# Key-value sums on column strips, spread on row strips, and rows transposed 32 at a time on four row strips of TensorE

## The chip, the cores and the metric

The kernel runs on one core of a Trainium2 chip. The core has TensorE for matmuls (PE in the profile, its weight loads PEld), VectorE (DVE), ScalarE (ACT), GpSimd (POOL) and SyncE (SP), which here only starts transfers. Matmuls read SBUF and write PSUM, which has eight banks of 128 partitions by 512 float32. The metric is the device time of one execution, in microseconds; lower is better.

## The reference

The kernel computes two identical layers on x of 2048 rows by 512 (bfloat16): attention with a softmax feature map, without a matrix of rows by rows, then a gated feed-forward part.

```
def A(x, wqkv, w_phi, wo):                 # 32 heads of 16
    q, k, v = split(x @ wqkv)
    pq, pk = q @ w_phi, k @ w_phi          # head by head
    phi_q = concat(softmax(pq), softmax(-pq))
    phi_k = concat(softmax(pk), softmax(-pk))
    kv, z = sum_s phi_k * v, sum_s phi_k
    num = phi_q @ kv
    den = phi_q @ z + 1e-6
    return (num / den) @ wo
def B(x, W_gate, W_up, W_down):            # 512 -> 1376 -> 512
    return (relu(x @ W_gate) * (x @ W_up)) @ W_down
for layer in range(2):
    x = x + A(layernorm(x))
    x = x + B(layernorm(x))
```

## The kernel before

The rows stay in SBUF (`x_sb`) as 16 tiles of 128 rows, worked in four blocks (`st`) of four tiles. Python code lists all operations with what they read and write and an assumed cost. `Program.schedule` then replays them greedily, choosing the order on each engine and a PSUM bank for each `bank(...)`, and `plan` sets the semaphore waits. The order is thus a result of the assumed costs, `occ` and `lat` in nanoseconds; it is fixed in the program, and each engine runs its list in order.

The steps, by function:

- `layernorm(st)` takes statistics on DVE (L435, L436), scales the rows to `ytile` (on DVE at L452; with `early` on ACT at L449) and turns every tile with four 128x128 transposes (helper `tr`, L327) into one bank, which is copied to `yT` in one go: on ACT at L463, with `early` on DVE at L460. There are 15 calls that work on four tiles at once (`step` 4) and one, the very first, that works tile by tile.
- `keys(st)` multiplies each transposed tile by the key and the value weights (`mm`, L323), takes both exponentials on ACT (L487), their sums by head on DVE (L489, L491), and on POOL (L498) makes `vhat`, the values times the reciprocal sums with one column more per head for z, so 17 columns a head. The key-value sums come next: for each of eight groups `g` (sign by quarter of the features) a 128x128 slice of `expk` is multiplied by the 136 columns of `vhat` of its eight heads, over the four tiles: 32 matmuls of 136 columns into three banks. Only the products of a head with itself are wanted, so most of each 128x136 block is not used. Three DVE operations add the banks to `kvsum` (L511, L514).
- `sums()` runs once a layer: it masks `kvsum` into `ZDw` (the weights of the denominators, L523) and `kvbd` (L529), eight DVE operations each.
- `queries(st)` makes `expq` (L539). `attend(st)` computes denominators with 32 matmuls of 16 columns (`ZDw`, `expq`), then the factors `atok`, transposed to `aT`, which must be spread from one row per head to the head's 16 rows. For block 0 this is done on TensorE, with eight matmuls by the constant `EC`; half of the results are multiplied into `expq` on DVE straight from PSUM (L586), the other half by way of a copy on ACT (L590, L591). For the other blocks it is a round trip through DRAM: one write to `scratch` (L575) and eight reads into `abT` (L577) on SP's queue. The numerators are 32 matmuls on 32x32 tiles of the array (L600), copied to `oT`, multiplied by `wo_sb` and added to `x_sb`.
- `glu(st)` is the feed-forward part: matmuls by `Wg`, `Wu` and `Wd`, relu on ACT (L639), product on DVE (L641), residual on DVE (L624).

The first layer's keys of all four blocks come first. Then, per layer, `glu` of one block runs between `out_of_a` of the next one and, in the first layer, `into_a` of the same block for the second layer.

Of the kernel before, what the change touches and what calls it, by code (L numbers as in the profile page):

```python
# [246 lines left out]
def build_kernel(nc, A_x, A_wqkv, A_w_phi, A_wo, W_gate, W_up, W_down, out):  # L247
# [8 lines left out]
    with ExitStack() as ctx:  # L256
# [4 lines left out]
        def sb(name, shape, dt=BF16):  # L261
            return E(nc.sbuf_tensor(name, [P] + list(shape), dt))

        NWARM = 8
        NY, NYT, NE, NV, NG, NH = 4, 6, 5, 4, 3, 18
# [17 lines left out]
        kvsum = sb("kvsum", [8, 136], FP32)  # L283
        kvbd = sb("kvbd", [2, NC, 128])
# [16 lines left out]
        EC = sb("EC", [8, 128])  # L301
        ident = sb("ident", [128])
        mask8a = sb("mask8a", [8])
        mask8 = sb("mask8", [8])
        abT = sb("abT", [8, 512])
        scratch = [nc.dram_tensor(f"spread{i}", (64, 512), BF16, kind="Internal").ap() for i in range(2)]
# [72 lines left out]
        for i in range(NWARM):  # L379
# [8 lines left out]
        op("act", lambda e: e.activation(EC[:].rearrange("p g (h j) -> p (g h) j", j=16), ident[:, 0:64].unsqueeze(2).to_broadcast([P, 64, 16]), ACT.Copy),  # L388
           reads=[R("ident"), R("tables")], writes=[R("EC")], occ=1000, name="EC")

        op("dve", lambda e: e.tensor_tensor(BD.rearrange("p c (h f) -> p c h f", f=16),
# [34 lines left out]
        VIA = lambda c, sg: sg == 1  # L426

        def layernorm(st, step=4, early=False):

            b = cnt["yT"] % NYT  # L430
            cnt["yT"] += 1
            for t0 in range(4 * st, 4 * st + 4, step):
# [9 lines left out]
                if early:  # L442
                    op("dve", (lambda t0: lambda e: e.scalar_tensor_tensor(nmr[:, t0:t0 + step, :], mv[:, t0:t0 + step, 0:1], -1.0, rstd[:, t0:t0 + step, :], ALU.mult, ALU.mult))(t0),
                       reads=Rmv + Ry, writes=[R("nmr", t) for t in ts], occ=75, lat=165, name="nmr")
                for t in ts:
                    yb = cnt["y"] % NY
                    cnt["y"] += 1
# [3 lines left out]
                    else:  # L451
                        op("dve", (lambda t, yb: lambda e: e.tensor_scalar(ytile[:, yb, :], x_sb[:, t, :], mv[:, t, 0:1], rstd[:, t, :], op0=ALU.subtract, op1=ALU.mult))(t, yb),  # L452
                           reads=[R("x", t), R("mv", t), R("rs", t)], writes=[R("y", yb)], occ=322, lat=405, name=f"apply{t}", port=True)
                    ps = bank(f"ytr{t}")
# [4 lines left out]
                    if early:  # L459
                        op("dve", (lambda ps, dst: lambda e: e.tensor_copy(dst, b16half(ps).rearrange("p (c n) -> p c n", c=NC)))(ps, dst),  # L460
                           reads=[ps], writes=[R("yT", b, tt)], occ=331, lat=415, name=f"ycp{t}")
                    else:
                        op("act", (lambda ps, dst: lambda e: e.activation(dst, b16half(ps).rearrange("p (c n) -> p c n", c=NC), ACT.Copy))(ps, dst),  # L463
                           reads=[ps], writes=[R("yT", b, tt)], occ=480, lat=600, name=f"ycp{t}")
            return b

# [3 lines left out]
        def keys(st, b):  # L470

            tiles = []
            for tt in range(4):
                t = 4 * st + tt
                ry = R("yT", b, tt)
# [6 lines left out]
                for ic in range(NC):  # L482
                    mm(pk, full, yT[:, b, ic, tt * 128:(tt + 1) * 128], Wkp[:, ic, :], ic == 0, ic == NC - 1, [ry, R("W", "k", ic)], 512, f"k{t}")
                for ic in range(NC):
                    mm(pv, full, yT[:, b, ic, tt * 128:(tt + 1) * 128], wv[:, ic, :], ic == 0, ic == NC - 1, [ry, R("wv")], 512, f"v{t}")
# [15 lines left out]
            for g0, g1 in ((0, 3), (3, 6), (6, 8)):  # L501
                ps = bank(f"kv{st}{g0}")
                for g in range(g0, g1):
                    sg, c = g // 4, g % 4
                    for j, i in enumerate(tiles):
                        mm(ps, (lambda o: lambda p: p.f32()[:, o:o + 136])((g - g0) * 136), expk[:, i, sg, c * 128:(c + 1) * 128],
# [239 lines left out]
```

## Time and profile before

| | us |
|---|---|
| runs | 424.61, 426.39, 426.71 (median 426.39) |
| the profiled execution, in all | 424.71 |
| its span, first to last instruction | 423.0 |

| group | count | busy us, mean ns of one |
|---|---|---|
| DVE adds to `kvsum`, 408 columns and 272 columns | 12 and 6 | 6.9, 576 and 2.6, 431 |
| DVE writes of `ZDw` and of `kvbd` | 16 and 16 | 1.6, 163 and 3.4, 291 |
| `yT` copies on ACT and on DVE | 52 and 12 | 27.2, 608 and 4.6, 411 |
| spread matmuls (`aT`, `EC`) | 16 | 4.2, 383 |
| write to `scratch`, 64 KB | 6 | lands in 2.0 (median) |

A group's busy time can hold overlaps: matmuls are pipelined, so the next one starts while the last is still draining, and the distance from start to start is shorter than the mean duration. "32\*32" behind an operation is the part of the array that it uses, rows by columns. The granted clock is TensorE's, with 1.00 as full speed.

### The profile page before, as it was taken

What the parts mean: (1) busy time and instruction counts of PE and PEld (TensorE: products, weight loads), DVE (VectorE), ACT (ScalarE), POOL (GpSimd) and SP (SyncE); (2) the same over time, 40 slices, a digit from 0 to 9 for tenths busy, and PEclk for the clock granted to TensorE, in tenths of its full rate; (3) what the DMA queues carried; (4) which work ended last, traced back from release to release, by engine and by line L of the source; (5) the groups of instructions that cost most, each with busy time, mean ns of one, the idle gap of its engine ahead of it and who ended that gap; (6) DMA issues with size and microseconds to landing.
All of it is one profiled execution on the core that took longest, in us unless ns stands there. A gap on an engine that the chain in (4) does not pass through costs nothing.

```text
span 423.0 us, 6858 instructions
## 1 busy us (share of the span) xinstructions
PE 402.1 (95%) x2684; PEld 205.1 (48%) x2731; DVE 275.3 (65%) x587; ACT 213.6 (50%) x432; POOL 69.3 (16%) x71
## 2 busy tenths in 40 slices
PE   7999999599999999999999999977999999999997
PEld 4555555354444545455455445533444544444443
DVE  4999768968479647767774446876932842664332
ACT  5999897655246522834183169855522430342320
POOL 0258780000007000620052008000000000000000
PEclk9999999989999999999999999969999999999999
DMA  8960000330000000200000000022101001301001
GB/s 265 326 210 2 2 0 7 102 107 0 2 0 2 0 2 10 97 0 2 0 2 0 2 2 2 8 99 70 39 1 50 2 0 50 108 2 37 14 0 50
DMA packets 16800, 17.66 MB, mean 42 GB/s; under 512 B 1568, under 2 KB 15744, under 8 KB 16768
## 3 DMA queue, kind: packets, MB, share of 16 engines
q1 hardware_dynamic: 15552, 16.62, 12.0%
q10 hardware_dynamic: 1216, 0.61, 0.5%
q8 instruction: 21, 0.34, 0.3%
q14 instruction: 11, 0.09, 0.1%
HBM read 14.73 MB, written 2.49 MB: 41 GB/s over the span
## 4 chain that ended last, share of the span: by engine, by line
PE 76%; ACT 15%; DVE 6%; DMA 1%; issue 1%; ACTq 0%; DVEq 0%
PE pb L323 72%; ACT expq L539 4%; ACT expk L487 3%; PE pb L327 3%; ACT ytile L449 2%; ACT vsb L495 2%; DMA hT<-in_A_wqkv_dram 1%; DVE expq L591 1%; ACT yT L463 1%; DVE stats L435 1%; PE pb L600 1%; DVE expq L586 1%; DVE Zk L489 1%; ACT Wqp L420 0%; ACT abT L590 0%
## 5 line engine op out<-in xcount | busy, mean ns | idle before, releaser
L639 ACT ACTIVATE gate_sb<-pb 128x512 bf16<-128x512 f32 (+1 forms) x88 | 52.8, 600 | 130.3 <-PE pb L323 130.2
L498 POOL TENSOR_TENSOR vhat<-vsb,rZk 128x544 bf16<-128x544 bf16 x64 | 68.5, 1105 | 193.5 <-DVE rZk L491 187.1
L641 DVE TENSOR_TENSOR hT<-gate_sb,pb 128x512 bf16<-128x512 bf16 (+1 forms) x88 | 59.6, 683 | 52.6 <-PE pb L323 52.3
L323 PE MATMUL pb<-yT,Wu 128*128 128x512 bf16 (+1 forms) x345 | 91.1, 379 | 0.2
L323 PE MATMUL pb<-yT,Wg 128*128 128x512 bf16 (+1 forms) x341 | 90.6, 379 | 0.6
L323 PE MATMUL pb<-Wd,hT 128*128 128x512 bf16 (+3 forms) x355 | 76.8, 372 | 0.4
L624 DVE TENSOR_TENSOR x_sb<-x_sb,pb 128x512 bf16<-128x512 bf16 x55 | 36.4, 685 | 48.6 <-PE pb L323 48.6
L323 PEld LDWEIGHTS pb<-Wd,hT 128*128 128x128 bf16 (+1 forms) x363 | 35.4, 98 | 40.1
L323 PEld LDWEIGHTS pb<-yT,Wu 128*128 128x128 bf16 (+1 forms) x352 | 34.9, 100 | 38.4 <-issue 0.4
L323 PEld LDWEIGHTS pb<-yT,Wg 128*128 128x128 bf16 (+1 forms) x352 | 34.4, 100 | 38.1 <-issue 1.4
L435 DVE BATCH_NORM_STATS2 stats<-x_sb 128x6 f32<-128x512 bf16 x64 | 42.4, 680 | 2.2 <-ACT x_sb L619 1.4
L489 DVE TENSOR_REDUCE Zk<-expk 128x64 f32<-128x1024 bf16 x32 | 38.4, 1204 | 7.7 <-ACT expk L487 7.5
L539 ACT ACTIVATE expq<-pb 128x512 bf16<-128x512 f32 x64 | 35.0, 696 | 12.9 <-PE pb L323 12.9
L487 ACT ACTIVATE expk<-pb 128x512 bf16<-128x512 f32 x64 | 36.3, 639 | 2.3 <-PE pb L323 0.7
L323 PE MATMUL pb<-wo_sb,oT 128*128 128x512 bf16 x121 | 31.9, 399 | 2.2 <-DVE oT L608 1.7
L323 PE MATMUL pb<-wv,yT 128*128 128x512 bf16 x124 | 33.1, 379 | 0.3
L323 PE MATMUL pb<-Wkp,yT 128*128 128x512 bf16 x124 | 32.2, 379 | 0.4 <-DVE yT L460 0.2
L323 PE MATMUL pb<-yT,Wqp 128*128 128x512 bf16 x122 | 30.9, 379 | 0.4 <-ACT Wqp L420 0.2
L463 ACT ACTIVATE yT<-pb 128x512 bf16<-128x512 bf16 x52 | 27.2, 608 | 6.3 <-PE pb L327 6.2
L610 ACT ACTIVATE oT<-pb 128x512 bf16<-128x512 f32 x28 | 15.1, 609 | 24.4 <-PE pb L600 23.6
L591 DVE TENSOR_TENSOR expq<-expq,abT 128x512 bf16<-128x512 bf16 x56 | 21.9, 424 | 8.1 <-DMA abT<-spread 8.1
L323 PE MATMUL pb<-vhat,expk 128*128 128x136 bf16 x256 | 24.4, 223 | 0.2
(68 smaller groups left out, 327.4 us busy)
## 6 DMA issues: line engine op xcount, KB each, us to landing
abT<-spread SPq DMA_DIRECT2D x48, 128.0 KB
out_dram<-x_sb SPq DMA_DIRECT2D x15, 128.0 KB, 1.7
x_sb<-in_A_x_dram SPq DMA_DIRECT2D x3, 512.0 KB, 8.8
Wg<-in_B_W_gate_dram SPq DMA_DIRECT2D x1, 1376.0 KB
Wu<-in_B_W_up_dram SPq DMA_DIRECT2D x1, 1376.0 KB
Wd<-in_B_W_down_dram SPq DMA_DIRECT2D x1, 1280.0 KB
hT<-in_A_wqkv_dram ACTq DMA_DIRECT2D x2, 256.0 KB, 5.8
wv<-in_A_wqkv_dram SPq DMA_DIRECT2D x1, 512.0 KB, 5.8
```

What stands on the lines that cost most here:

```text
L323: op("pe", lambda e: e.matmul(view(ps), lhsT, rhs, start=start, stop=stop), reads=reads, writes=[ps], occ=max(25.0, 0.4167 * n + 2.6), lat ...
L435: op("dve", (lambda t: lambda e: e.bn_stats(stats[:, t, :], x_sb[:, t, :]))(t), reads=[R("x", t)], writes=[R("st", t)], occ=580, lat=680, ...
L463: op("act", (lambda ps, dst: lambda e: e.activation(dst, b16half(ps).rearrange("p (c n) -> p c n", c=NC), ACT.Copy))(ps, dst), reads=[ps], ...
L487: op("act", (lambda i, s, pk: lambda e: e.activation(expk[:, i, s, :], full(pk), ACT.Exp, scale=1.0 - 2.0 * s))(i, s, pk), reads=[pk], wri ...
L489: op("dve", (lambda i, zb: lambda e: e.tensor_reduce(Zk[:, zb, :], expk[:, i, :, :].rearrange("p s (h f) -> p (s h) f", f=16), AX.X, ALU.a ...
L498: op("pool", (lambda i, s, vb, rz: lambda e: e.tensor_tensor(vhat[:, i, s, :, :], vsb[:, vb, :, :], rZk[:, rz, s * 32:(s + 1) * 32].unsque ...
L539: op("act", (lambda c, s, ps: lambda e: e.activation(expq[:, st, c, s, :], full(ps), ACT.Exp, scale=1.0 - 2.0 * s))(c, s, ps), reads=[ps], ...
L591: op("dve", (lambda c, sg, gi: lambda e: e.tensor_tensor(expq[:, st, c, sg, :], expq[:, st, c, sg, :], abT[:, gi, :], ALU.mult))(c, sg, gi ...
L610: op("act", (lambda i, pn: lambda e: e.activation(oT[:, g, i, :], full(pn), ACT.Copy))(i, pn), reads=[pn], writes=[R("oT", g, i)], occ=480 ...
L624: op("dve", lambda e: e.tensor_tensor(x_sb[:, t, :], x_sb[:, t, :], full(ps), ALU.add), reads=[R("x", t), ps], writes=[R("x", t)], occ=597 ...
L639: op("act", (lambda m, gb, pg: lambda e: e.activation(gate_sb[0:m, gb, :], pg.f32()[0:m, :], ACT.Relu))(m, gb, pg), reads=[pg], writes=[R( ...
L641: op("dve", (lambda m, gb, hb, pu: lambda e: e.tensor_tensor(hT[0:m, hb, :], gate_sb[0:m, gb, :], pu.f32()[0:m, :], ALU.mult))(m, gb, hb, pu),
```

## The change

**Key-value sums.** The array is used as four column strips of 32. A strip multiplies the 32 features of two heads by the 34 columns of `vhat` of these two heads, so each 136-column product becomes four of 34 columns, which write 32 partitions each of one bank. All eight groups fit in that bank (272 columns), one operation adds it to `kvsum`. There are 128 matmuls a block, issued as two runs of 64 for two tiles each. `kvsum` shrinks to 8x34 columns and `kvbd` to 32 columns a group.

**Sums.** Three DVE operations in place of sixteen: the epsilon, all of `ZDw`, all of `kvbd`.

**Transposes.** For calls with four tiles, `strips` turns 32 rows of a tile at a time: the four row strips of the array each take their 32 partitions of `ytile` and write to a bank of their own. This makes 64 transposes to 128x32 in one run that starts when all four tiles are scaled, and four copies to `yT`, two on ACT and two on DVE (with `early` four on DVE). A copy holds one strip of all four tiles, so keys of any tile wait for all four. `ytile` has eight buffers in place of four.

**Spread.** `atok` is laid out with 32 columns a quarter, so that `aT` has a quarter's factors on its own 32 partitions. For block 0, the four quarters of one sign are spread at once by four row strips into four banks. The copy by way of ACT is now taken for odd quarters, where it was taken for one sign. The scratch write of the other blocks is all 128 rows of `aT` (128 KB).

```diff
-        NY, NYT, NE, NV, NG, NH = 4, 6, 5, 4, 3, 18
+        NY, NYT, NE, NV, NG, NH = 8, 6, 5, 4, 3, 18
-        kvsum = sb("kvsum", [8, 136], FP32)
-        kvbd = sb("kvbd", [2, NC, 128])
+        kvsum = sb("kvsum", [8, 34], FP32)
+        kvbd = sb("kvbd", [2, NC, 32])
-        EC = sb("EC", [8, 128])
+        EC = sb("EC", [2, 128])
...
-        VIA = lambda c, sg: sg == 1
+        by_tile = set()
+        VIA = lambda c, sg: c % 2 == 1
...
+                    if step == 4:
+                        continue
...
+                if step == 4:
+                    strips(st, b, ybs, early)
             return b
+
+        def strips(st, b, ybs, early):
+            pss = [bank(f"ytr{st}{i}") for i in range(4)]
+            def turn(e):
+                for tt, yb in enumerate(ybs):
+                    for c in range(NC):
+                        for i in range(4):
+                            r = slice(32 * i, 32 * i + 32)
+                            n0 = c * 128 + tt * 32
+                            ins = e.transpose(pss[i].b16()[:, n0:n0 + 32], ytile[r, yb, c * 128:(c + 1) * 128], ident[r, r], tile_position=(32 * i, 0))
+                return ins
+            op("pe", turn, reads=[R("y", yb) for yb in ybs] + [R("ident")], writes=pss, occ=600, lat=800, name=f"ytr{st}")
+            for i in range(4):
...
+                if early or i % 2:
+                    op("dve", (lambda src, dst: lambda e: e.tensor_copy(dst, src()))(src, dst), reads=[pss[i]], writes=[R("yT", b, i), R("ya", b, i)], occ=331, lat=415, name=f"ycp{st}")
+                else:
+                    op("act", (lambda src, dst: lambda e: e.activation(dst, src(), ACT.Copy))(src, dst), reads=[pss[i]], writes=[R("yT", b, i), R("ya", b, i)], occ=480, lat=600, name=f"ycp{st}")
...
-                ry = R("yT", b, tt)
+                ry = [R("yT", b, tt)] + [R("ya", b, i) for i in range(4)] if b in by_tile else R_yT(b)
...
-            for g0, g1 in ((0, 3), (3, 6), (6, 8)):
-                ps = bank(f"kv{st}{g0}")
-                for g in range(g0, g1):
-                    sg, c = g // 4, g % 4
-                    for j, i in enumerate(tiles):
-                        mm(ps, (lambda o: lambda p: p.f32()[:, o:o + 136])((g - g0) * 136), expk[:, i, sg, c * 128:(c + 1) * 128],
-                           vhat[:, i, sg, c * 8:(c + 1) * 8, :], j == 0, j == 3, [R("ek", i, sg), R("vh", i, sg)], 136, f"kv{st}")
...
+            ps = bank(f"kv{st}")
+            def products(js):
+                def fn(e):
+                    for j in js:
+                        for g in range(8):
+                            sg, c = g // 4, g % 4
+                            for i in range(4):
+                                f0 = c * 128 + 32 * i
+                                ins = e.matmul(ps.f32()[32 * i:32 * i + 32, g * 34:g * 34 + 34], expk[:, tiles[j], sg, f0:f0 + 32],
+                                               vhat[:, tiles[j], sg, 8 * c + 2 * i:8 * c + 2 * i + 2, :], start=j == 0 and g == 0, stop=j == 3,
+                                               skip_group_check=True, tile_position=(0, 32 * i))
+                    return ins
+                return fn
+            for js in ((0, 1), (2, 3)):
+                op("pe", products(js), reads=[...],
+                   writes=[ps], occ=500, lat=700, name=f"kv{st}")
...
+            op("dve", lambda e: e.tensor_scalar(kvv[:, 0:4, :, 16], kvv[:, 0:4, :, 16], float(EPS_DEN), None, op0=ALU.add),
+               reads=[R("kvs")], writes=[R("kvs")], occ=70, lat=160, name="eps z")
...
-                dma("sp", lambda e: e.dma_start(scr, aT[0:64, g, :]), reads=[R("aT", g)], writes=[rs], nbytes=65536, name=f"aTo{st}")
+                dma("sp", lambda e: e.dma_start(scr, aT[:, g, :]), reads=[R("aT", g)], writes=[rs], nbytes=131072, name=f"aTo{st}")
...
+        def spread(g, sg):
+            pss = [bank(f"ab0{c}{sg}") for c in range(NC)]
+            def products(e):
+                for c in range(NC):
+                    r = slice(32 * c, 32 * c + 32)
+                    ins = e.matmul(full(pss[c]), EC[r, sg, :], aT[r, g, :], start=True, stop=True, tile_position=(32 * c, 0))
+                return ins
+            op("pe", products, reads=[R("EC"), R("aT", g)], writes=pss, occ=450, lat=650, name="ab0")
+            for c in range(NC):
+                scale_by(0, c, sg, pss[c])
```

## The prediction

> **What bounds the kernel now.** First the page's engine totals and its slices, then busy time by stretch of the span.
>
> ```profile
> span 423.0 us, 6858 instructions
> PE 402.1 (95%) x2684; PEld 205.1 (48%) x2731; DVE 275.3 (65%) x587; ACT 213.6 (50%) x432; POOL 69.3 (16%) x71
> PEclk9999999989999999999999999969999999999999
> ```
>
> ```profile
> 30.00:70.00 40.00, 39.44 (x358) 23.26 (x362) 32.27 (x69) 35.24 (x72) 25.61 (x24) 1.00 0.01 1
> 90.00:270.00 180.00, 178.88 (x1136) 90.88 (x1156) 120.95 (x239) 85.04 (x170) 34.28 (x32) 1.00 0.04 12
> 290.00:420.00 130.00, 128.80 (x693) 61.10 (x704) 64.96 (x126) 40.52 (x76) 0.00 (x0) 1.00 0.10 33
> 70.00:90.00 20.00, 14.77 (x164) 8.07 (x165) 15.79 (x47) 15.38 (x35) 0.00 (x0) 0.91 0.22 72
> 270.00:290.00 20.00, 15.10 (x160) 7.15 (x160) 16.57 (x48) 13.34 (x32) 0.00 (x0) 0.83 0.18 60
> ```
>
> The columns of a stretch are PE, PEld, DVE, ACT, POOL, then granted clock, DMA share and GB/s. In three stretches, 350 of 423 us, TensorE is busy for 99% of the time at full clock, and the starts of its 512-column matmuls lie 0.216 us apart with hardly a gap (four in 0.86 us). There every TensorE nanosecond added or removed moves the end one for one, and what DVE, ACT or POOL gain is worth nothing. Only around 70 to 90 and 270 to 290 us, where a layer's first query block waits for DVE and ACT, does TensorE idle, some 5 us each; before 30 us it idles too. So I count TensorE time, then waits.
>
> The two kinds of work that the change splits are these groups:
>
> ```profile
> L323 PE MATMUL pb<-vhat,expk 128*128 128x136 bf16 x256 | 24.4, 223 | 0.2
> L327 PE MATMUL pb<-ident,ytile 128*128 128x128 bf16 x256 | 22.7, 228 | 1.5 <-DVE ytile L452 1.2 <-DVE kvsum L511 0.2
> L323 PE MATMUL pb<-ZDw,expq 128*128 128x16 bf16 x256 | 9.1, 170 | 3.6 <-ACT expq L539 3.6
> L600 PE MATMUL pb<-expq,kvbd 32*32 32x512 bf16 x256 | 5.6, 409 | 4.2 <-DVE expq L591 4.2
> ```
>
> Their mean durations overlap, so a price is the distance between starts, from the instructions in order of time:
>
> ```profile
> 62.74 0.93 PE L323 MATMUL pb<-vhat,expk 128*128 128x136 bf16 x13
> 63.51 0.38 PE L323 MATMUL pb<-yT,Wqp 128*128 128x512 bf16 x1
> 65.76 2.42 PE L323 MATMUL pb<-ZDw,expq 128*128 128x16 bf16 x90
> ...
> 75.96 0.52 PEld L323 LDWEIGHTS pb<-ZDw,expq 128*128 128x128 bf16 x18 [0.33 <-ACT expq L539]
> 76.50 0.33 PEld L600 LDWEIGHTS pb<-expq,kvbd 32*32 32x32 bf16 x32
> ...
> 121.14 0.19 PEld L600 LDWEIGHTS pb<-expq,kvbd 32*32 32x32 bf16 x32 [0.43 <-issue]
> 121.14 0.65 PE L600 MATMUL pb<-expq,kvbd 32*32 32x512 bf16 x32
> 121.73 0.39 PE L323 MATMUL pb<-yT,Wg 128*128 128x512 bf16 x1
> ...
> 335.14 0.61 PE L327 MATMUL pb<-ident,ytile 128*128 128x128 bf16 x8
> 335.59 0.38 PE L323 MATMUL pb<-yT,Wg 128*128 128x512 bf16 x1
> ```
>
> A key-value product costs (63.51 - 62.74) / 13 = 0.059 us, a transpose (335.59 - 335.14) / 8 = 0.0565, and a 16-column product, the shortest here, (2.42 - 0.17) / 89 = 0.0253.
>
> **Two prices that decide.** (1) The 32 tiled products of L600 are the only tiled ones. The matmul ahead of the run at 121.14 starts at 120.83 and streams until 121.05, so going in costs 0.09 us. Half of its products stream after the other half, the last starts at 121.42 and streams until 121.63, and the next plain matmul starts at 121.73: 0.09 to 0.10 going out. Other runs of L600 in the busy stretches show the same. I take 0.18 us for each change into a tiled form and back. (2) At 121.14, after long matmuls, the 32 weight loads start 3.3 ns apart (0.19 us less one load's 0.09, over 31). At 76.50, after 18 short pairs, the same 32 need 0.33 us: by their single starts the first 28 come 3.3 ns apart and the last four 34 ns apart, with nothing late that they depend on. Around 277.4 us, again after short pairs and with the clock at half, it is 28 quick ones and then 34 ns. I read this as a store of ready instructions, at least 29 pairs of load and matmul deep when full, refilled at one pair in 34 ns whatever the TensorE clock. Against 512-column matmuls the refill is never seen; a long run of short pairs empties the store and then goes at 34 ns. The 90 pairs at 65.76 don't contradict it: 29 + 2.25 / 0.034 = 95.
>
> **The change, part by part.**
>
> Key-value sums: in each of 8 blocks 32 products of 136 columns (32 x 0.059 = 1.89 us) become 128 products of 34 columns, in two runs of 64. By (1) and (2) a run takes 0.18 + (64 - 29) x 0.034 = 1.37 us. 16 x 1.37 - 8 x 1.89 = **+6.8 us**. The trace has no run of 64 tiled pairs, so bounds: from below every pair at the quick 3.3 ns but four tiles at a time sharing the 25.3 ns step, 64 x 0.0063 + 0.18 = 0.58 us a run, -5.8 in all; from above 25.3 ns for every pair, 64 x 0.0253 + 0.18 = 1.80, +13.7. I take 1.37 because the late loads at 76.50 are tiled ones in just this situation.
>
> Transposes: in 15 four-tile calls 16 transposes (0.90 us) become 64 of 32 rows. Twelve stand alone in the new order: 12 x 1.37 = 16.4. One follows a key-value run directly and finds the store empty: 64 x 0.034 + 0.09 = 2.27. Two follow another such run together: 128 x 0.034 + 0.09 = 4.44. Total 23.1, less 15 x 0.90 = 13.5: **+9.6 us**. Bounds as above: 15 x 0.58 - 13.5 = -4.8, and 15 x 1.80 - 13.5 = +13.5.
>
> Store not refilled: in two places of layer one only four 512-column matmuls stand between a key-value run and a transpose run (0.86 us refills 25 pairs, 4 are used, 8 lack: 0.27 each), and the first layer's 128 denominator products come three matmuls after a run (16 pairs ready; 62 x 0.0253 + 66 x 0.034 = 3.8 instead of 3.2). **+1.1**, between 0 and 2.
>
> New waits: keys now need all four row strips, where the first key tile needed one transposed tile. In the first layer no TensorE work stands between the strips of block 1 and its keys, so TensorE waits for the matmul's tail and four DVE copies of 0.41 us (0.35 from start to start): **+1.7** (0 to 3, as DVE has key sums of 1.2 us in its queue, and behind TensorE's keys ACT's exponentials wait). In four other places eight 512-column matmuls (1.73 us) cover 0.2 us of tail and two copies on each engine, 2 x 0.61 on ACT; cover gone, 1.5 us each. **+0.5** (0 to 3). Behind the wide copies, relu and residuals queue, with slack in the busy stretches.
>
> Sums and spread: before, eight ZDw writes (0.163), eight kvbd writes (0.21 from start to start) and three kvsum adds; after, one add, three short steps. DVE loses some 2 us at each layer's start, but kvbd isn't what zm waits for. TensorE waits for kvsum, eps and ZDw in a row, about 1.2 us, with three matmuls (0.65 us) as cover instead of five: **+0.3** (-1 to +1). Eight spread matmuls (1.7 us a layer) become two passes of about 0.4, but DVE's eight products behind them, four of 0.68 and four of 0.42 us, are unchanged and end last: **0** (-1.5 to +0.5). The wider scratch write is 128 KB; output writes of 128 KB land in 1.7 us and this one of 64 KB in 2.0, so **0**. Mask constants are made while the first weights load: 0. Of the 48 wide copies to yT that ACT had in these calls, 24 go to DVE, 24 x 0.41 = 10 us, against some 8 us of kvsum adds that it loses; in TensorE's stretches neither counts (DVE is busy for 121 of 180 us, ACT for 85).
>
> Absorbed: between 20 and 30 us DVE is busy for 10.00 and ACT for 9.97 of 10 us, TensorE for 9.02, and the first runs fall there: **-1.0**.
>
> 6.8 + 9.6 + 1.1 + 1.7 + 0.5 + 0.3 - 1.0 = **+19.0 us**. The profiled execution took 424.71 us with a span of 423.0; 424.71 + 19.0 = 443.7. The median of the runs is 426.39, 1.7 above that execution, so I say **444**.
>
> **Rivals.**
> *The strips really overlap* (faster). If the 34 ns belonged to something else around 76 us, runs cost 0.58: -5.8 - 4.8 + 1.7 + 0.5 + 0.3 - 1.0 = -9.1, 416 us. For it: full runs of L600 load at 3.3 ns. Against: both runs after short pairs fall to 34 ns at the same load. It decides from a run below 0.87 us on: (15.1 + 13.5 - 1.5 of small terms) over 31 runs. [...]
> *A fixed step per matmul.* If pairs in four tiles don't overlap at all, 25.3 ns each: 13.7 + 13.5 + 1.7 + 0.5 + 0.3 - 1.0 = +28.7, 453 us. For it: no sustained run in the trace is quicker. Against: L600. [...]
> *The clock.* TensorE's granted clock was 0.51 from 85.5 to 88.0 after 2 us of idling. If the sparse runs and the wait around block 1 halve it for three spells like that of 3.4 us, 3 x 1.7 = 5 us come on top: 449.
> *It comes out even*: DVE's relief shortens both 20-us stretches by as much as TensorE loses, 426. DVE is busiest there (15.8 and 16.6 of 20), but its chain keeps its eight long products.
>
> **Chances.** Forecast 0.58 (434 to 450 by the bounds of the small terms and a refill of up to 39 ns, which the 90 pairs still allow with 32 ready), fixed step 0.16, clock 0.09, overlap 0.13, even 0.04. A measurement of this kernel tells about 0.5% from no change. Slower 0.58 + 0.16 + 0.09 = 0.83 and a share of the even case, 0.84; faster 0.13; the same 0.03. The range 430 to 455 leaves out the overlap case and the ends of the others.
>
> **What would show it.** Right: runs of x64 on the 32x34 and 128x32 forms about 1.2 us long, their loads 34 ns apart after about 29, a gap of 0.09 us before and after, TensorE still at 95% or more. Wrong: runs of 0.5 us, or loads 25 ns apart from the first; or TensorE idle time well above 25 us, which would make waits and not the runs the cause.

## The result, and the profile after

The changed kernel takes 430.73 us (median of 4 runs, 429.84 to 433.09), the kernel before in the same session 425.5 (4 runs, 424.23 to 426.71): 1.0125 times the time, 95% interval 1.0084 to 1.0165. It is slower, as forecast, but by 5.3 us and not by 19. Its profiled execution took 430.46 us.

First the totals on the page of the kernel after, with the clock granted in the 40 slices:

```profile
span 428.7 us, 9857 instructions
PE 400.1 (93%) x4219; PEld 190.9 (45%) x4219; DVE 272.1 (63%) x571; ACT 202.4 (47%) x408; POOL 69.2 (16%) x71
PEclk9989699579999999999999999958999999999999
```

TensorE runs 4219 matmuls in place of 2731 (the trace before holds 2684 of them, and all 2731 weight loads), and yet it is busy for 2 us less. What grew is its idle time: 428.7 - 400.1 = 28.6 us, where it was 423.0 - 402.1 = 20.9, part of which stands for the missing records. The clock row has new dips at the third and the fifth digit, and deeper ones from the eighth on and in layer two. Busy time by stretch of the kernel after (PE, PEld, DVE, ACT, POOL, then clock, DMA share, GB/s) says where:

```profile
20.00:30.00 10.00, 6.26 (x215) 3.36 (x213) 8.97 (x27) 9.74 (x21) 4.45 (x5) 0.96 0.76 266
30.00:55.00 25.00, 21.54 (x326) 9.80 (x325) 12.90 (x21) 19.60 (x39) 10.73 (x10) 0.81 0.01 2
75.00:100.00 25.00, 18.08 (x302) 9.30 (x299) 20.57 (x60) 13.07 (x31) 0.00 (x0) 0.73 0.30 102
100.00:265.00 165.00, 165.00 (x1614) 77.34 (x1612) 110.91 (x214) 69.30 (x139) 26.99 (x26) 1.00 0.03 8
```

From 30 to 70 us the kernel before had TensorE busy for 39.44 of 40 us at a clock of 1.00. Now, from 30 to 55, it idles 3.5 us of 25, and the mean clock is 0.81. The long stretch from 100 us on is as full as it was.

The times at which certain matmuls start cut both spans into the same stretches. "Queries" is everything from the last `Wd` matmul of the first layer to the second layer's first denominator product (`ZDw`):

| stretch, us | before | after | difference |
|---|---|---|---|
| start to first `ZDw` | 64.53 | 74.53 | +10.00 |
| to first `Wg` (first feed-forward) | 24.53 | 26.00 | +1.47 |
| to last `Wd` of layer one | 156.66 | 151.16 | -5.50 |
| queries of layer two | 19.63 | 23.03 | +3.40 |
| `ZDw` to first `Wg`, layer two | 26.06 | 26.33 | +0.27 |
| to the end | 131.57 | 127.66 | -3.91 |
| span | 422.98 | 428.72 | +5.74 |

Not all of these differences are gain or loss, because the new order moved work across the cuts. Counted by weight loads, 18 query matmuls of the first layer and 19 of the second stood behind the first `ZDw` product before and filled a wait there (18 x 0.216 = 3.9 us, 19 x 0.216 = 4.1); after, all 64 stand ahead of it. And 12 matmuls by `wo_sb` (2.6 us), with four small transposes of `atok` (0.2), left each feed-forward stretch for the one ahead of it. Without what moved, the six differences are about +6.1, +2.5, -2.7, -0.7, +1.6 and -1.1 us. So the stretches in which TensorE is full gained 4.5 us, about what the cheaper runs in them would give (4.2 us by the prices found below), and most of the loss is in the first layer's key stage; the two stretches behind a first `ZDw` lost 4.1 us together.

The groups of the split work, in the kernel after (count | busy, mean ns | idle before):

```profile
L542 PE MATMUL pb<-vhat,expk 128*32 128x34 bf16 x1024 | 10.6, 182 | 2.6 <-POOL vhat L530 2.5
L487 PE MATMUL pb<-ident,ytile 32*128 32x32 bf16 x960 | 10.1, 177 | 2.9 <-ACT expq L576 1.3 <-issue 0.8 <-DVE kvsum L553 0.8
L325 PE MATMUL pb<-ZDw,expq 128*128 128x16 bf16 x256 | 7.3, 170 | 0.4 <-DVE ZDw L562 0.4
```

1024 key-value products are busy for 10.6 us, where 256 wider ones took 24.4. A run between plain matmuls, in order of time:

```profile
59.09 0.38 PE L325 MATMUL pb<-Wkp,yT 128*128 128x512 bf16 x1
59.40 0.66 PE L542 MATMUL pb<-vhat,expk 128*32 128x34 bf16 x64
60.00 0.82 PE L325 MATMUL pb<-Wkp,yT 128*128 128x512 bf16 x3
```

From 59.09 to 60.00 is 0.91 us, less 0.216 for the first matmul itself: 0.69 us a run, the median of all 16 as well. A strip transpose run costs 0.68 by the same reckoning. The forecast was 1.37 for either. By the single starts, some 32 pairs start four in 27 ns, the others 8.4 ns apart; going in costs the forecast 0.09, and from the last start to the next plain matmul it is 0.11 to 0.12.

Now the key stage of the kernel after, TensorE in order of time with the idle time ahead of a group and what ended it:

```profile
25.88 0.66 PE L542 MATMUL pb<-vhat,expk 128*32 128x34 bf16 x64 [1.17 <-POOL vhat L530]
27.36 0.65 PE L487 MATMUL pb<-ident,ytile 32*128 32x32 bf16 x64 [0.81 <-DVE kvsum L553]
29.58 1.89 PE L325 MATMUL pb<-Wkp,yT 128*128 128x512 bf16 x4 [1.57 <-DVE yT L495]
...
40.66 1.69 PE L325 MATMUL pb<-yT,Wqp 128*128 128x512 bf16 x7
43.69 0.66 PE L542 MATMUL pb<-vhat,expk 128*32 128x34 bf16 x64 [1.35 <-POOL vhat L530]
44.29 0.65 PE L487 MATMUL pb<-ident,ytile 32*128 32x32 bf16 x64
46.24 0.44 PE L487 MATMUL pb<-ident,ytile 32*128 32x32 bf16 x36 [1.30 <-ACT expq L576]
47.50 0.38 PE L487 MATMUL pb<-ident,ytile 32*128 32x32 bf16 x28 [0.82 <-issue]
47.81 1.89 PE L325 MATMUL pb<-Wkp,yT 128*128 128x512 bf16 x4
49.49 1.91 PE L325 MATMUL pb<-wv,yT 128*128 128x512 bf16 x4
...
74.53 3.64 PE L325 MATMUL pb<-ZDw,expq 128*128 128x16 bf16 x128 [0.39 <-DVE ZDw L562]
```

and ACT at the same time:

```profile
28.10 2.91 ACT L459 ACTIVATE ytile<-x_sb,nmr,rstd 128x512 bf16<-128x512 bf16 x4
```

In the kernel before, block 2's transposes and its keys came much earlier, and the first `ZDw` product with them:

```profile
35.63 0.39 PE L327 MATMUL pb<-ident,ytile 128*128 128x128 bf16 x4
...
37.05 0.59 PE L323 MATMUL pb<-Wkp,yT 128*128 128x512 bf16 x2
...
64.53 0.25 PE L323 MATMUL pb<-ZDw,expq 128*128 128x16 bf16 x4
```

Three things are to be seen. Block 2's rows are all scaled at 31.0 us, but its transposes stand in TensorE's list behind block 1's key-value sums, so they start at 44.29, after a wait for POOL, and those of block 3 stand directly behind them, where they wait for four PSUM banks (`expq` on ACT empties them). Then, four 512-column matmuls take 1.89 us instead of 1.03: half clock, at 29.6 and again from 47.8 us (the granted clock is 0.50 from 29.3 to 32.7 and from 46.4 to 53.2). And there is an idle 0.82 us in the middle of a run, which no semaphore explains.

### The profile page after: what moved, and what is told of

The parts are those of the page before. It is cut to its first block, busy times and chain, and to the rows that moved or that the text cites. A ratio compares the mean times of both kernels' runs of the same rounds, so it can differ in the third digit from the quotient of the medians.

```text
span 428.7 us, 9857 instructions
## 1 busy us (share of the span) xinstructions
PE 400.1 (93%) x4219; PEld 190.9 (45%) x4219; DVE 272.1 (63%) x571; ACT 202.4 (47%) x408; POOL 69.2 (16%) x71
## 4 chain that ended last, share of the span: by engine, by line
PE 83%; DVE 9%; ACT 5%; DMA 1%; issue 1%; ACTq 0%; DVEq 0%
PE pb L325 78%; DVE stats L443 2%; PE pb L487 2%; PE pb L542 2%; DMA hT<-in_A_wqkv_dram 1%; ACT expq L576 1%; ACT expk L519 1%; DVE expq L661 1%; DVE expq L656 1%; PE pb L630 1%; DVE Zk L521 1%; ACT ytile L459 1%; DVE zm L595 1%; ACT oT L640 1%; ACT vsb L527 0%
## 5 line engine op out<-in xcount | busy, mean ns | idle before, releaser
L325 PE MATMUL pb<-yT,Wu 128*128 128x512 bf16 (+1 forms) x352 | 92.7, 379 | 0.0
L325 PE MATMUL pb<-Wd,hT 128*128 128x512 bf16 (+2 forms) x363 | 77.4, 372 | 0.0
L679 DVE TENSOR_TENSOR x_sb<-x_sb,pb 128x512 bf16<-128x512 bf16 x55 | 36.3, 685 | 46.8 <-PE pb L325 46.7
L576 ACT ACTIVATE expq<-pb 128x512 bf16<-128x512 f32 x64 | 33.3, 663 | 11.4 <-PE pb L325 11.0
L325 PE MATMUL pb<-Wkp,yT 128*128 128x512 bf16 x128 | 35.6, 403 | 1.6 <-DVE yT L495 1.6
L325 PE MATMUL pb<-wo_sb,oT 128*128 128x512 bf16 x128 | 34.1, 414 | 2.1 <-ACT oT L640 2.1
L325 PE MATMUL pb<-wv,yT 128*128 128x512 bf16 x128 | 34.8, 395 | 0.0
L325 PE MATMUL pb<-yT,Wqp 128*128 128x512 bf16 x128 | 29.5, 380 | 0.2 <-ACT Wqp L426 0.2
L325 PEld LDWEIGHTS pb<-wo_sb,oT 128*128 128x128 bf16 x128 | 12.8, 104 | 19.5 <-ACT oT L640 3.7
L527 ACT ACTIVATE vsb<-pb 128x512 bf16<-128x512 f32 x32 | 20.3, 634 | 1.1 <-PE pb L325 1.1
```

Source lines behind the costliest of these rows:

```text
L325: op("pe", lambda e: e.matmul(view(ps), lhsT, rhs, start=start, stop=stop), reads=reads, writes=[ps], occ=max(25.0, 0.4167 * n + 2.6), lat ...
L527: op("act", (lambda vb, pv: lambda e: e.activation(vsb[:, vb, :, 0:16], full(pv).rearrange("p (h d) -> p h d", d=16), ACT.Copy))(vb, pv), ...
L576: op("act", (lambda c, s, ps: lambda e: e.activation(expq[:, st, c, s, :], full(ps), ACT.Exp, scale=1.0 - 2.0 * s))(c, s, ps), reads=[ps], ...
L679: op("dve", lambda e: e.tensor_tensor(x_sb[:, t, :], x_sb[:, t, :], full(ps), ALU.add), reads=[R("x", t), ps], writes=[R("x", t)], occ=597 ...
```

## The experiments

Ratios are to the kernel before, run on the same chip in the same session, with 95% intervals. Medians of different sessions are not compared closely, since the kernel before itself took 425.1 to 426.5 us in them. All kernels start from the kernel after.

The times of stretches come from one execution of each kernel, and executions differ before the change can matter: the first key matmul (`Wkp`) starts at 10.2 to 13.2 us, although the kernels in the two tables run the same TensorE matmuls up to there. The last column therefore counts from that matmul; it is 77.16 us for the kernel before.

**Which part costs: no early strips, no strips, the old key-value sums, the old spread.**

```diff
 early_by_tile: strips only in the twelve calls that are not early
-            (by_tile.add if step < 4 else by_tile.discard)(b)
+            whole = step == 4 and not early
+            (by_tile.discard if whole else by_tile.add)(b)
...
-                if step == 4:
+                if whole:
                     strips(st, b, ybs, early)
 no_strips:  whole = False
 kv_old:     the 32 products of 136 columns and the sixteen sums of before, five ytile buffers
 spread_old: the eight 128-row products by EC and the 64 KB scratch write of before
```

> As changed, but the three first-layer calls of layernorm with early (blocks 1 to 3) turn each tile by four 128x128 transposes again, with a copy per tile. Theory A (the loss is waiting at the whole-block step in the first layer's key stage, where the first denominator product starts 10.0 us later than before, at 74.53 instead of 64.53 us): most of the 10 us come back, the first denominator product starts near 65 to 67 us, and the time falls from 430.7 to some 421 to 423 us, below the kernel before. Rival B (the key-value runs over two tiles, which wait for vhat of both, hold that stage up): little comes back, 428 to 431. Rival C (the prediction: the runs themselves cost TensorE more): the three calls have 3 x 0.2 us less or more, 430.

> As changed, but all 15 transposes by tile again; key-value strips and spread stay. Theory A: as early_by_tile in the key stage, but the twelve later transpose runs lose what they gain in the changed profile, 0.90 against 0.68 us each, 12 x 0.22 = 2.6 us: 424 to 426. Rival B: 430 to 433. Rival C: faster than early_by_tile by 12 x 0.46 = 5.5 us.

> As changed, but the key-value sums as before: 32 products of 136 columns a block, three adds, sixteen steps in sums (five ytile buffers, since eight don't fit beside the wide kvsum). Theory A: the stage stays late, and TensorE loses what the runs gain, 16 x 0.69 against 8 x 1.89 us, 4.1 us: 433 to 436. Rival B: the stage gains 5 us or more, 424 to 428.

> As changed, but the spread as before: eight 128-row products for block 0, one sign by way of ACT, scratch writes of 64 KB. Theory A: no part of the loss, 429.5 to 432. Rival D (the four-bank spread and the wider scratch write lengthen the stretches between the first denominator product and the first Wg, 26.0 and 26.3 us against 24.5 and 26.1 before): 1 to 3 us faster, 428 to 429.5.

| kernel | median us (runs) | ratio | start to `ZDw` | start to first `Wg` | `Wg` to last `Wd` | first `Wkp` to first `Wg` |
|---|---|---|---|---|---|---|
| after | 430.73 (4) | 1.0125 [1.0084, 1.0165] | 74.53 | 100.53 | 151.16 | 90.04 |
| early_by_tile | 421.62 (10) | 0.9903 [0.9873, 0.9934] | 66.55 | 93.56 | 151.17 | 80.46 |
| no_strips | 421.4 (9) | 0.9922 [0.9892, 0.9953] | 64.02 | 88.76 | 154.09 | 78.24 |
| kv_old | 433.24 (4) | 1.0187 [1.0144, 1.023] | 73.70 | 100.83 | 152.64 | 87.69 |
| spread_old | 427.06 (10) | 1.0054 [1.0025, 1.0084] | 69.27 | 96.17 | 151.16 | 85.27 |

The three early transposes (blocks 1 to 3 of the first layer) are the loss: without their strips the kernel is 9 us faster and faster than before. Taking back the key-value strips makes it 2.5 us slower still, so they are not the loss; their gain isn't shown by this run alone, since the intervals overlap and the kernel has fewer `ytile` buffers. The twelve other strip calls can't be told from nothing in the times, 0.9903 against 0.9922 (expected for no_strips were 424 to 426 us). In the stretches, 154.09 - 151.17 = 2.9 us are gained behind the first `Wg`, but 1.7 of them are eight `wo_sb` matmuls that moved ahead of it, which leaves 1.2, about six runs at 0.22; ahead of it, the last column is 2.2 longer with the strips, and without the moved matmuls 0.5.

**The spread and the late strips by themselves.** The old spread had saved 3.7 us, more than was expected for it, but nearly all of it in the key stage, where nothing is spread: the planner had put the operations in another order, with the early strip runs of blocks 2 and 3 apart. Three kernels part this.

```diff
 kv_only:                no_strips with the old spread
 late_strips_spread_old: early_by_tile with the old spread
 hold_late:              late_strips_spread_old, and 12 query matmuls of block 3 are held until block 0's denominators are in SBUF
-                       R_yT(b) + [R("W", "q", ic)], 512, f"q{st}")
+                       R_yT(b) + [R("W", "q", ic)] + [R("go")] * (st == 3 and c > 0), 512, f"q{st}")
```

> The kernel before with the key-value strips and the three-step sums alone: no row-strip transposes, spread as before. Theory A (strips cost by waiting, key-value runs at 0.69 us each gain 4.1 us): about 421.5 us. If the spread itself cost the 3.7 us by which spread_old was faster than the changed kernel (theory D), this is 3 us or more faster than no_strips (421.4), 418. If spread_old was faster because another order came out in the first layer's key stage (theory E: there its first denominator product starts 5.3 us earlier, while the stretches that hold the spread are not shorter, 26.9 against 26.0 us), it equals no_strips within 1 us.

> As early_by_tile (the three early calls by tile, the twelve later ones on strips), with the spread as before. Theory D: 418. Theory E: as early_by_tile, 421.6 within 1 us. The twelve strips' gain is in the two feed-forward stretches (151.2 and 127.7 us against 154.1 and 130.0 without them) and its price in the stretches before and after the denominators.

> As late_strips_spread_old, but twelve query matmuls of block 3 (three of four quarters) may start only when block 0's denominators are done, as thirteen query matmuls did in the kernel before. Theory F (with runs priced at 0.5 and 0.6 us the planner puts all 64 query matmuls ahead of the denominators, so none is left to fill TensorE's wait behind them): 2 to 5 us faster than late_strips_spread_old, with the query-to-denominator stretch of layer two near 20.5 instead of 23.0 us and the next one no longer. If that wait is set by ACT and DVE, which get the block's exponentials in it: the same or slower.

kv_only: 421.88 us (4 runs), 0.9865 [0.9824, 0.9906]; late_strips_spread_old: 422.74 (8), 0.9925 [0.9879, 0.9971]; hold_late: 423.93 (6), 0.9928 [0.9892, 0.9964]. With the early strips gone, the old spread makes no difference that these runs can tell (0.9922 and 0.9865 without strips, 0.9903 and 0.9925 with the late ones), so no gain or loss of the spread can be shown, and the 3.7 us are put down to the order. kv_only is the kernel before with the key-value strips and their shorter sums: that part of the change gains 1.35% on its own. Holding query matmuls back to fill the wait behind the denominators changed nothing, so whether the late strips lose for want of such cover is not shown by it.

**What makes a pair cost 34 ns.** The prediction's second price came from the last four loads at 76.50 in the kernel before. Its 18 short products ahead were each an operation with a semaphore increment of its own; the 64 of a strip run have one at the end. The kernel signals turns this round: its 128 key-value products a block are operations of their own, and the 32 denominator products a block are one:

```diff
-            for js in ((0, 1), (2, 3)):
-                op("pe", products(js), ...)
+            for j in range(4):
+                for g in range(8):
+                    sg, c = g // 4, g % 4
+                    for i in range(4):
+                        op("pe", (lambda j, g, sg, c, i, f0: lambda e: e.matmul(...))(j, g, sg, c, i, c * 128 + 32 * i), ...)
...
-                        mm(zd, ..., ZDw[:, sg, c, :].rearrange("p (q h) -> p q h", q=2), ...)
+            op("pe", dens, ..., writes=[zd], occ=810, lat=980, name=f"zd{st}")
```

> As changed, in the same order, but each of the 64 products of a key-value run signals its end (64 operations with a semaphore increment each instead of one), and the 32 denominator products of a block signal once. Theory S (34 ns is the price of a signal, not of a tiled pair): key-value runs fall to 34 ns a pair after some 30 pairs and take 1.2 to 1.4 us from change to change instead of 0.69, denominator runs stay at 25 ns to the end, where 31 of 128 came 34 ns apart; 436 to 441 us. Theory of the prediction (any short pair refills at 34 ns): the changed profile has already gone against it with 8.4 ns; then nothing changes here, 430 to 432.

443.36 us (4 runs), 1.0393 [1.0344, 1.0442]: 16.9 us above the kernel before in its session, where the kernel after was 5.2 above, so 11.6 us more, and more than the 436 to 441 that were expected. The order of work on every engine is that of the kernel after. A key-value run there, in order of time:

```profile
60.94 1.48 PE L539 MATMUL pb<-vhat,expk 128*32 128x34 bf16 x64
62.57 0.60 PE L325 MATMUL pb<-Wkp,yT 128*128 128x512 bf16 x2 [0.16 <-issue]
```

By single starts its first 32 pairs are as quick as ever and the other 32 come 34 ns apart, while the denominators, which now signal once, keep 25 ns from first to last. The run's last product starts at 62.24. The trace lacks some matmuls directly behind these runs (`Wkp` has 123 records of 128), so of the 0.33 us up to 62.57 I count 0.12 as going out, as in the kernel after; a run then costs 0.31 + 1.30 + 0.12 - 0.216 = 1.52 us in place of 0.69. 16 x 0.83 = 13.3 us, near the 11.6 measured. The 34 ns is the price of a pair that signals.

**Why the early strips cost: the wait for the block, the form, or the place in the order.** One kernel keeps transposes by tile but lets keys wait for all four tiles. The next keeps the order of the kernel after to the instruction and replaces the three runs of 64 by runs of 16 whole transposes in the same four banks. The next needs only two banks for such a run. The last keeps the strips and only makes the planner prefer them by 300 ns.

```diff
 early_wait_all (from early_by_tile)
-  ... if b in by_tile else R_yT(b)
+  ... if b in by_tile and st == 0 else R_yT(b)
 early_run_of_16
-            op("pe", turn, reads=..., writes=pss, occ=600, lat=800, name=f"ytr{st}")
+            op("pe", tiles if early else turn, reads=..., writes=pss, occ=600, lat=800, name=f"ytr{st}")
 early_run_of_16_two_banks: as that, and
-            pss = [bank(f"ytr{st}{i}") for i in range(4)]
+            pss = [bank(f"ytr{st}{i}") for i in range(2 if early else 4)]
 early_strips_sooner
-  ... writes=pss, occ=600, lat=800, name=f"ytr{st}")
+  ... writes=pss, occ=600, lat=800, name=f"ytr{st}", bonus=300.0 * early)
```

> This is early_by_tile (the three early calls of the first layer transpose by tile, 16 matmuls of 32x... per block), but the key matmuls of blocks 1 to 3 start only when all four tiles of their block are transposed and copied, as they do behind a strip run. Theory W (what costs in the first layer's key stage is the wait for the whole block): the stretch from the start to the first ZDw product goes from 66.6 us most of the way to the 74.5 of the kernel after, 70 to 75 us, and the time to 425 to 430. Theory R (it is the run of 64 transposes itself, with its four PSUM banks that come free together): the stretch stays at 66 to 68 us and the time at 421 to 423.

> The kernel after, with the three early runs of 64 strip transposes replaced by runs of 16 whole 128x128 transposes, in the same four banks, at the same assumed cost: the order of every engine stays that of the kernel after. Theory O (what costs is the place in the order: the run for block 2 stands behind block 1's key-value sums): the start to the first ZDw product takes 73.5 to 75.5 us and the time is 429 to 432. Theory R (the strip form costs): the stretch falls to 66 to 70 us and the time to 421 to 426.

> As early_run_of_16, but a run fills two PSUM banks, two tiles in each, in place of four; still one run a block, and the keys wait for all of it. The planner then puts the run of block 2 behind the keys of block 1 and ahead of their key-value sums, and no two runs are next to each other. If the four banks that must be free at once are what spoils the order, the start to the first ZDw product takes 65 to 68 us and the time is 421 to 424; if one run a block is enough to spoil it, 70 to 75 and 425 to 430.

> The kernel after with one number added: the planner prefers the early strip runs by 300 ns, which puts the run of block 2 amid the keys of block 1 and that of block 3 amid those of block 2. Strips, banks and copies stay. Theory O: the start to the first ZDw product falls from 74.5 to 64 to 68 us and the time to 419 to 424. Theory R: the stretch stays above 71 us and the time above 426.

| kernel | median us (runs) | ratio | start to `ZDw` | start to first `Wg` | first `Wkp` to first `Wg` |
|---|---|---|---|---|---|
| after | 430.73 (4) | 1.0125 [1.0084, 1.0165] | 74.53 | 100.53 | 90.04 |
| early_run_of_16 | 427.95 (4) | 1.0084 [1.006, 1.0108] | 71.32 | 98.21 | 86.19 |
| early_run_of_16_two_banks | 425.24 (10) | 1.0002 [0.9979, 1.0025] | 67.53 | 93.78 | 83.58 |
| early_wait_all | 423.49 (11) | 0.994 [0.9911, 0.9969] | 65.93 | 92.56 | 82.40 |
| early_by_tile | 421.62 (10) | 0.9903 [0.9873, 0.9934] | 66.55 | 93.56 | 80.46 |
| early_strips_sooner | 423.9 (10) | 0.999 [0.9968, 1.0012] | 68.08 | 94.99 | 82.78 |

The wait alone is not it: early_wait_all stays far from the kernel after. But it is a part: its key stage looks short only because its first key matmul starts 2.95 us sooner than that of early_by_tile. From that matmul on it needs 1.9 us more, and the ratios differ by 0.0037, or 1.6 us, with intervals that overlap. early_run_of_16 fell between its two theories, and its timeline shows why. It has the same order and nearly the same waits:

```profile
28.50 1.07 PE L495 MATMUL pb<-ident,ytile 128*128 128x128 bf16 x16 [0.81 <-DVE kvsum L564]
31.07 1.04 PE L325 MATMUL pb<-Wkp,yT 128*128 128x512 bf16 x4 [1.51 <-DVE yT L503]
...
44.40 1.07 PE L495 MATMUL pb<-ident,ytile 128*128 128x128 bf16 x16
46.35 1.07 PE L495 MATMUL pb<-ident,ytile 128*128 128x128 bf16 x16 [0.88 <-ACT expq L587]
47.25 1.03 PE L325 MATMUL pb<-Wkp,yT 128*128 128x512 bf16 x4
48.11 1.03 PE L325 MATMUL pb<-wv,yT 128*128 128x512 bf16 x4
...
71.32 3.64 PE L325 MATMUL pb<-ZDw,expq 128*128 128x16 bf16 x128 [0.39 <-DVE ZDw L573]
```

Four matmuls take 1.03 where they took 1.89 behind the strips, and its busy time from 30 to 55 us is the same at full clock:

```profile
30.00:55.00 25.00, 21.55 (x244) 11.00 (x245) 16.87 (x29) 23.50 (x46) 12.17 (x12) 1.00 0.01 1
```

From the keys of block 2 on (47.81 and 47.25) up to `ZDw`, it needs 24.07 us against 26.72. That 2.65 is the second spell of half clock. From the first key matmul to these keys it needs 35.22 us against 37.32; in these 2.1 lie the first spell and the idle 0.82. Together the key stage gained 4.7 us, counted from its first key matmul. In the time of the whole kernel less of that is seen, 1.0084 against 1.0125, and the intervals overlap.

The strip transposes by themselves don't bring the half clock. kv_old has the same strip runs, with waits of 0.90 and 1.57 us around the first, but key-value products of 136 columns, and there the clock is 1.00 from 14 to 78 us and four matmuls take 1.04 us behind the strips. Its first `ZDw` product is late all the same (73.70).

What is left is the wait and the order. With two banks a run no longer has to find four banks free, and the planner puts block 2's directly behind block 1's keys:

```profile
35.88 1.06 PE L495 MATMUL pb<-ident,ytile 128*128 128x128 bf16 x16
36.77 1.89 PE L325 MATMUL pb<-yT,Wqp 128*128 128x512 bf16 x8
38.59 0.67 PE L553 MATMUL pb<-vhat,expk 128*32 128x34 bf16 x64
39.19 1.47 PE L325 MATMUL pb<-yT,Wqp 128*128 128x512 bf16 x6
40.50 1.03 PE L325 MATMUL pb<-Wkp,yT 128*128 128x512 bf16 x4
```

The query matmuls now stand between transposes and keys and cover the copies, and block 2's keys start at 40.50. Half clock is gone in this stage (1.00 from 22 to 69.8 us), and so is the wait of 1.35 us for POOL. Of what was expected of this run, the stretch came out as for the theory of the four banks (67.53) and the time as for the other (425.24). early_strips_sooner confirms the order from the other side, with the strips untouched:

```profile
31.30 1.88 PE L325 MATMUL pb<-Wkp,yT 128*128 128x512 bf16 x4 [1.57 <-DVE yT L495]
...
35.68 0.65 PE L487 MATMUL pb<-ident,ytile 32*128 32x32 bf16 x64
37.24 1.04 PE L325 MATMUL pb<-wv,yT 128*128 128x512 bf16 x4 [0.91 <-ACT expk L519]
...
43.25 0.65 PE L487 MATMUL pb<-ident,ytile 32*128 32x32 bf16 x64
```

The run of block 2 comes at 35.68 instead of 44.29, only the first spell of half clock is left (a mean of 0.87 and 0.63 in the two stretches from 28.83 to 35.65 us), and the kernel is 1.3% faster than the kernel after, some 5.7 us (its interval, 0.9968 to 1.0012, lies wholly below that of the kernel after). Its first `ZDw` product has 16 query matmuls less ahead of it, so for this kernel the last column is the one to compare.

Put together, from early_by_tile to the kernel after, by the ratios and then by the last column: keys wait for the whole block, 1.6 and 1.9 us; one run a block in two banks, 2.6 and 1.2; the same in four banks and with the order of the kernel after, 3.5 and 2.6; strips in place of whole transposes in that order, 1.7 and 3.9. Each of these steps but the last also lets the planner choose another order. That the order counts is shown, since the intervals of two banks and four, and of early_strips_sooner and the kernel after, don't touch. The first and the last step are not shown by the times alone.

**Strips only where TensorE is full.** Nine calls have other TensorE work around them; the others go by tile.

```diff
-            buf[st] = layernorm(st, step, early)
+            buf[st] = layernorm(st, step, early, not early and st < 3)
...
-            return layernorm(st)
+            return layernorm(st, covered=st > 0)
 covered_strips_so: the same with the old spread
```

> The kernel after, but strips only in the nine calls in whose stretch TensorE had no idle time (the second normalization of blocks 1 to 3 in both layers, and the first one of the second layer for blocks 0 to 2); the early calls, and the calls that open a stretch of waiting or close it, go by tile. Theory C (a strip run gains where TensorE is full, and loses only where something waits for its block): the key stage is that of early_by_tile, the second layer's query stage is 21 us as without strips, and the time is 417 to 419.5 us, under no_strips' 421.4 by the 2 to 4 us that the full stretches gain. Rival (what the full stretches gain is given back at their end, since the next dependent stretch then has less work left to cover it): 421 to 422.5 us, with TensorE idle for the difference between the last product of a full stretch and the ZDw products or the second layer's queries.

> covered_strips with the old spread and its 64 KB scratch write. If the spread is worth nothing beside the order of the early stage (kv_only stood as no_strips), its time is that of covered_strips within 1 us: 417 to 420 by theory C, 421 to 422.5 by the rival. If the new spread costs on its own, it is faster than covered_strips by 1 to 3 us.

covered_strips: 421.73 us (5 runs), 0.9888 [0.9842, 0.9934], so the rival's time, and no gain over no_strips (0.9922) that these runs can tell. Its stretch from `Wg` to the last `Wd` is 152.90 us and its last one 129.39, against 154.09 and 129.99 without strips, but the second layer's stretch from `ZDw` to `Wg` is 0.7 longer. The key stage is 0.5 longer only by its start; from the first key matmul on both need 53.51. covered_strips_so: 419.34 (5 runs), 0.9848 [0.9809, 0.9888], the fastest of all, with a key stage of 62.33 us. It beats the kernel before and the kernel after; against kv_only (0.9865) the intervals overlap, so it is not shown that its strips are what helps.

## Why the prediction was right in sign and wrong in size

- **Key-value sums, +6.8, and transposes, +9.6.** Both mis-sized, with the wrong sign. The step that failed is price (2), "a store of ready instructions [...] refilled at one pair in 34 ns", carried over "because the late loads at 76.50 are tiled ones in just this situation". They were in another situation: behind 18 products that signal. Runs took 0.69 and 0.68 us, so 16 x 0.69 = 11.0 against 15.1 is -4.1, and 15 x 0.68 = 10.2 against 13.5 is -3.3. The lower bound (0.58) was near, and the first rival's mechanism, strips that really overlap, held: 8.4 ns a pair. Where every product signals, the traces show 34 ns a pair, on strips (the second half of a key-value run in signals) and on the whole array (the last 29 denominators of layer one in the kernel after) alike.
- **Mode change, 0.18 a run.** Right: 0.09 in, 0.11 to 0.12 out with the last product itself.
- **Store not refilled, +1.1.** The denominators behind a run did slow down, from 25 ns to 34 for the last 29 of 128 in layer one and the last 32 in layer two (about 0.3 us each), but as products that signal; a transpose run behind a key-value run did not (8.5 ns a pair in the one at 44.29).
- **New waits, +1.7 and +0.5.** This is where the time went. The places were named (the keys of block 1: 1.57 us idle, as worked out), but the price stopped at the wait itself. The sum took the place of each run from the new order and charged its pairs, never asking how long its rows had been ready: block 2's waited for 13 us, and its keys with them. The key stage grew by 10.0 us, 6.1 without the query matmuls that moved into it, though its own eight key-value and three transpose runs together got shorter. Against early_by_tile, the early runs cost 9.4 us by the ratios.
- **The clock rival, +5.** The half clock is there, and its size: the key stage has a granted clock of 0.50 for 3.4 us around 31 and for 6.8 us around 50, as long as the three spells of 3.4 it spoke of. early_run_of_16 puts their cost between 1.7 us (by the ratios) and 4.7 (in the key stage). Behind the first `ZDw` there are 13.7 us more at half clock (0.50 from 77.1 to 90.7 us), where before there were 3.4 (85.5 to 89.0); what these cost is not shown. I had priced it on top of runs that were too dear, and so it seemed a variant of the slow case rather than the loss itself.
- **Sums +0.3, spread 0, wider scratch write 0.** The spread came out at nothing. The write landed in 3.3 us and not in 2.0, and no kernel shows a cost of it. The sums were too dear: from the first `ZDw` to the first numerators it takes 12.0 us before and 11.3 in kv_old, both with sixteen steps, and 10.4 in the kernel after.
- **Absorbed, -1.0.** Wrong way round: between 20 and 30 us TensorE was busy for 9.02 and is now for 6.26.
- **The sum.** 430.73 lies just inside the range (430 to 455) and below the forecast's own 434 to 450. The right sign is luck: the runs, which were to make the kernel slower, by themselves make it faster, and the sign came out of two errors that go opposite ways: 23.8 us too much for the runs (16.4 forecast, -7.4 found), and 10.5 too little for all else (2.6 forecast; 5.7 + 7.4 = 13.1 found by the spans). My last sentence on what would show it wrong, TensorE idle well above 25 us, is what the page then showed: 28.6. One slip beside it: the times of the first two rivals, 416 and 453, are counted from the profiled execution (424.71), and those of the forecast and the others from the median, 1.7 higher; nothing hangs on it.

## What to carry to other kernels

The split matmuls paid here because a whole run signals once: 64 tiled pairs of 34 columns took 0.69 us with one signal and 1.52 with 64. But an operation that takes four of eight PSUM banks at once goes where a greedy planner finds four free, and here that was 13 us behind its data: for each operation that is made larger, compare when its inputs are ready with when it starts, in the new order, before pricing its instructions. And a stretch between two marks changes its length when work moves across a mark, or when the execution starts late: 5.2 us of what the two feed-forward stretches seemed to gain had only moved, so count the matmuls in a stretch before comparing its time.

## What the runs showed of the hardware

- Pairs of load and matmul with a semaphore increment each came 34 ns apart late in a run (34 columns on strips in signals, 16 columns on the whole array in the kernel after); pairs without came 8.4 ns apart (34 columns on strips, kernel after) or 25 (16 columns on the whole array, signals). On strips the first 32 pairs of a run show nothing of the 34 ns, nor do the first 99 (layer one) and 96 (layer two) of the 128 denominators in the kernel after, which start 25 ns apart.
- Between the same waits, 64 strip transposes were followed by half clock (kernel after: a mean of 0.57 from 28.83 to 32.24 us, 0.57 and 0.50 in the two stretches from 45.89 to 52.72) and 16 whole transposes were not (early_run_of_16: 1.00 in the same stretches). It was so at both places where the two kernels can be compared. With key-value products of 136 columns in place of the strip runs (kv_old) the same strip transposes kept 1.00; why is not shown.
- The 0.82 us gap inside a run at 46.7 us stays unexplained; it came once in 15 transpose runs.
